# Block-sparse attention and FFN on one core: V's matmuls of DMA-turned visits moved to mid-step, queries on another queue

## The chip, the cores and the metric

The kernel runs on one core of one Trainium2 chip. The metric is the device time of one execution in microseconds, lower is better. PE, DVE, ACT and POOL are the compute engines (TensorE, VectorE, ScalarE, GpSimd); SP only issues DMAs here.

## The reference

For 4 batches, 8 heads, 768 positions and head size 64, attention is computed under a mask of 32 x 32 blocks: neighbours, the first and the last block row and column, and three sampled blocks per block row. The result, as 512 channels per position, goes through a layer norm, an FFN of 512 to 2048 to 512 with relu, and a residual.

```python
scores = np.where(mask, scale * q @ k.T, -1e9)
attn = np.exp(scores - scores.max(-1)); attn /= attn.sum(-1) + 1e-9
x = (attn @ v).transpose(0, 2, 1, 3).reshape(B, S, H * D)
xn = (x - mean) / np.sqrt(var + 1e-6) * g_ln
out = x + np.maximum(xn @ w_ch1, 0) @ w_ch2
```

## The kernel before

Each batch has six tiles of 128 queries, 24 tiles in all. A tile is worked through in visits: five tiles of a batch are one job "N" of two visits (four heads each, 256 gathered keys per block row); the tile with the edge blocks has a job "H" of one visit and a job "D" (dense rows) of four, where visits 0 and 1 are the two key halves of one set of heads, and 2 and 3 of the other. In order of work a batch is N, N, N, H, D, N, N: 15 visits, 60 in all, numbered through.

The main loop makes one step per visit (lines 564 to 620). In step s the scores of visit s run on PE (`scores`, L206) and their maximum on DVE (`biggest`, L242); then the V matmuls of the visit before, `pvi` (`attn_v`, L293), with their division on DVE (`evict`, L335 to L348); then the exponentials of visit s on ACT (`softmax`, L256). P has to be turned before V's matmuls. Either PE turns it within the step (`turn`: L283, copied out of PSUM by ACT, L284). Or, for visits marked `by_dma`, ACT and POOL split P in two f16 halves (L260, L261), SP issues two DMA transposes (`turn_begin`, L268), and in the next step DVE adds the turned halves (`turn_end`, L272). Marked are, from visit 9 on, the second half of the visits of N and D jobs.

FFN matmuls fill the rest of PE's time. A unit of two tiles (the first and the last unit have one) has 192 first-layer matmuls (L386; relu into f16 halves by ACT, L396, and DVE, L397) and 96 second-layer ones (L410), as f16 products in three terms, in three PSUM tiles. `run(amount)` emits matmuls up to a planned amount in ns (`yield c1`, 109 for two tiles, and `yield 215`). A unit may begin three steps after its last visit; `budget` spreads what is left over the steps until the next unit begins. The other work of a step is a list of tasks, and `run(budget / (len(tasks) + 1))` stands ahead of each: in the first visit of a job the next job's query load (`load_q`, L173, when it begins a tile), key steps (`keys`, on SP: one window load, then twelve gathers of 64 KB in four groups, L155) and V loads (`values`, L183 and L191 on ACT from job 7 on, else SP, and four gathers on POOL, L195); in the first steps the splitting of the weights (L441 to L452); then `turn`, and last `norms` (layer norm, and x turned by DMA transposes on SP, L367 xth and L368 xtl). Keys and V have two buffers each, so a load of V for the next job waits for the V matmuls of the job before this one.

Where `pvi` is a DMA visit, 2600 ns of FFN stand ahead of its V matmuls and beyond the budget:

```python
            if pvi.by_dma:
                turn_end(pvi)
                run(2600)
            attn_v(pvi)
```

Engines execute in the order in which the code emits to them, each queue for itself.

Of the kernel before, what the change touches and what calls it, by code (L numbers as in the profile page):

```python
# [25 lines left out]
def sparse_attention_moe(  # L26
# [13 lines left out]
    nc = tc.nc  # L40
# [7 lines left out]
    NX, LAG, FFN0 = 5, 1, 3  # L48
    LIFT = 2048.0
    BY_DMA = 9  # L50
# [8 lines left out]
    def ring(name, n, shape, dtype):  # L59
        return [const.tile(shape, dtype, name=f"{name}{i}") for i in range(n)]  # L60
# [10 lines left out]
    q_s = ring("q", 2, [P, 4, P], F32)  # L71
# [98 lines left out]
            nc.gpsimd.tensor_copy(kv[:, 0:n, s, :], src[:, m : m + 1, :].to_broadcast([P, n, P]))  # L170

    def load_q(n):
        nc.sync.dma_start(q_s[n % 2], qT[tiles[n].b, tiles[n].t])  # L173

    def values(job):
        src, vs = v[job.b], job.vs
# [76 lines left out]
    def softmax(vi):  # L253
        n, w = vi.shape
        for h in range(n):
            nc.scalar.activation(p_s[:, h * w : (h + 1) * w], seen(vi)[:, h, :], AF.Exp,  # L256
                                 bias=vi.st[:, 4 + h : 5 + h], scale=0.125)
            if vi.by_dma and (h + 1) % (n // 2) == 0:
                part = slice((h + 1 - n // 2) * w, (h + 1) * w)
                nc.scalar.copy(ph_s[:, part], p_s[:, part])  # L260
                nc.gpsimd.tensor_sub(pl_s[:, part], p_s[:, part], ph_s[:, part])  # L261
        if vi.kind == "D" and vi.r:
            nc.scalar.activation(vi.st[:, 12:16], vi.st[:, 8:12], AF.Exp)
# [6 lines left out]
    def turn_end(vi):  # L270
        c = vi.shape[0] * vi.shape[1] // P
        nc.vector.tensor_add(pt_s[vi.i % 2][:, 0:c, :], pth_s[:, 0:c, :], ptl_s[:, 0:c, :])  # L272
# [13 lines left out]
    def attn_v(vi):  # L286
        pt, vs = pt_s[vi.i % 2], vi.job.vs
        pv = vi.pv = ps_v.tile([P, 512], F32, tag="pv", name=f"pv{vi.i}")
        nch = 3 if vi.kind == "D" else 2
        begun = set()  # L290

        def mm(row, col, ch, vv, e, c):
            nc.tensor.matmul(pv[32 * row : 32 * row + 32, 65 * col : 65 * col + 65],  # L293
                             pt[:, ch, 32 * row : 32 * row + 32], vs[:, vv, 65 * e : 65 * e + 65],
                             start=row not in begun, stop=c == nch - 1, skip_group_check=True)
            begun.add(row)

        if vi.kind == "N":
            for h in vi.heads:
                for c in range(2):  # L300
                    for gg in range(4):
                        mm(gg, h % 4, (2 * (h % 2) + h % 4 // 2) * 2 + c, 2 * gg + c, h, c)
        elif vi.kind == "H":
            for pp in range(2):
                for j in range(2):
                    for c in range(2):
                        for rr in range(2):
                            h = 4 * pp + 2 * rr + j
                            for gg in range(2):
                                mm(2 * rr + gg, 2 * pp + j, (2 * j + pp) * 2 + c,  # L310
                                   2 * gg + c, h, c)
        else:
            for j in range(2):
                for c in range(3):
                    for rr in range(2):
                        for gg in range(2):
                            mm(2 * rr + gg, j, 3 * j + c, 3 * vi.r + c, 4 * vi.hf + 2 * rr + j, c)

    def evict(vi):
        n = 2 if vi.kind == "D" else 4  # L320
        u = vi.pv[:, 0 : n * 65].rearrange("p (h e) -> p h e", e=65)
        if vi.kind == "D":
            half = sm.tile([P, 2, 65], F32, tag="half", name=f"half{vi.i}")
            if not vi.r:
                nc.vector.tensor_copy(half, u)
                vi.half = half
                return
            wt = vi.st[:, 12:16].rearrange("p (r h) -> p r h", r=2).unsqueeze(3)
            nc.vector.tensor_mul(half, u, wt[:, 1].to_broadcast([P, 2, 65]))
            both = vi.mate.half  # L330
            nc.vector.tensor_mul(both, both, wt[:, 0].to_broadcast([P, 2, 65]))
            nc.vector.tensor_add(half, half, both)
            u = half
        rs = sm.tile([P, n, 1], F32, tag="rs", name=f"rs{vi.i}")
        nc.vector.tensor_scalar(out=rs, in0=u[:, :, D : D + 1], scalar1=1e-9 * LIFT,  # L335
                                scalar2=None, op0=ALU.add)
        nc.vector.reciprocal(rs, rs)
        x = vi.tile.x
        if vi.kind == "N":
            o = x[:, vi.hf * 256 : vi.hf * 256 + 256].rearrange("p (h d) -> p h d", d=D)  # L340
            nc.vector.tensor_mul(o, u[:, :, 0:D], rs.to_broadcast([P, 4, D]))
            return
        for rr in range(2):
            rows = slice(64 * rr, 64 * rr + 64)
            for pp in range(n // 2):
                h = 4 * (vi.hf if vi.kind == "D" else pp) + 2 * rr
                o = x[64:128, h * D : (h + 2) * D] if vi.kind == "D" else x[0:64, h * D : (h + 2) * D]
                nc.vector.tensor_mul(o.rearrange("p (j d) -> p j d", d=D),  # L348
                                     u[rows, 2 * pp : 2 * pp + 2, 0:D],
                                     rs[rows, 2 * pp : 2 * pp + 2, :].to_broadcast([64, 2, D]))  # L350
# [116 lines left out]
    tiles, units, visits = [], [], []  # L467
# [4 lines left out]
    n = 0  # L472
    while n < len(tiles):
        k = 1 if n == 0 or n == len(tiles) - 1 else 2
# [28 lines left out]
            for r in (1, 3):  # L503
                jobs[-1].visits[r].mate = jobs[-1].visits[r - 1]
    for vi in visits:
        vi.by_dma = vi.i >= BY_DMA and vi in vi.job.visits[len(vi.job.visits) // 2 :] and vi.kind != "H"
    NV = len(visits)
    NLAST = visits[-1].i

# [33 lines left out]
    def run(amount):  # L543
        while queue and (amount > 0 or queue[0].left <= 0):
            cost = next(queue[0].gen, None)
            if cost is None:
                queue.pop(0)
                continue
            if cost < 0:
                break  # L550
            queue[0].left -= cost
            amount -= cost

    def norms():
        for t in tiles:
# [3 lines left out]
            if t.normed is not None and t.spread is None:  # L559
                if t.u.i < 2 or units[t.u.i - 2].up_done:  # L560
                    norm_b(t)
                    t.spread = s

    while s < NV + LAG + 2 or queue or nextu < len(units):
        assert s < NV + 60
        vi = visits[s] if s < NV else None
        pvi = visits[s - LAG] if 0 <= s - LAG < NV else None
        if vi:
            scores(vi)
            biggest(vi)  # L570
        if pvi:
            t = pvi.tile
            if pvi is t.visits[0]:
                assert t.n < NX or tiles[t.n - NX].done
            if pvi.by_dma:
                turn_end(pvi)
                run(2600)
            attn_v(pvi)
            evict(pvi)
            if pvi is t.visits[-1]:  # L580
                t.ready = True
        if vi:
            softmax(vi)
            if vi.by_dma:
                turn_begin(vi)
        while nextu < len(units) and units[nextu].at <= s:
            u = units[nextu]
            if any(t.spread is None or t.spread >= s for t in u.tiles):
                break
            u.gen = ffn(u)  # L590
            u.left = 192 * (84, 109)[len(u.tiles) - 1] + 48 * 215 * len(u.tiles)
            queue.append(u)
            nextu += 1
        budget = 0
        if queue:
            left = sum(u.left for u in queue)
            budget = left / (max(1, units[nextu].at - s) if nextu < len(units) else 1)
        tasks = [(fn, args) for fn, args in todo.pop(s, [])]
        if vi:
            nxt = jobs[vi.job.i + 1] if vi is vi.job.visits[0] and vi.job.i + 1 < len(jobs) else None  # L600
            pre = []
            if nxt:
                gen = keys(nxt)
                pre = [(load_q, (nxt.visits[0].tile.n,))] if nxt.visits[0] is nxt.visits[0].tile.visits[0] else []
                pre += [(next, (gen, 0)), (values, (nxt,))] + [(next, (gen, 0))] * 6
            tasks = pre + tasks
            if queue:
                k = len(tasks) // 2
                tasks = tasks[:k] + [(turn, (vi,))] + tasks[k:]
            else:  # L610
                tasks = [(turn, (vi,))] + tasks
        tasks.append((norms, ()))
        for fn, args in tasks:
            run(budget / (len(tasks) + 1))
            fn(*args)
        if queue:
            want = sum(u.left for u in queue) - (left - budget)
            run(want)
        norms()
        s += 1  # L620
# [51 lines left out]
```

## Time and profile before

| | before |
|---|---|
| median of 3 runs | 835.66 us (835.5 to 836.88) |
| profiled execution | 833.35 us |
| its span, first to last instruction | 831.6 us |
| busy PE, DVE, ACT, POOL | 84%, 42%, 34%, 31% |
| TensorE clock granted, mean | 0.933 |

The profiled execution takes 1.75 us more than its span. In the profile's rows a line such as L293 is a line of the kernel; a row of the timeline has start, duration, engine, line, operation, output and input, and in brackets the idle time ahead of it and what ended it. Granted clock 1.00 is 2.4 GHz, 0.50 is 1.2 GHz.

### The profile page before, as it was taken

How to read it: one execution, taken by the hardware profiler on the slowest of the kernel's cores; microseconds unless marked ns; L12 is line 12 of the kernel's file. 1: busy time of each engine (PE TensorE's matmuls, PEld its weight loads, DVE VectorE, ACT ScalarE, POOL GpSimd, SP SyncE). 2: the span in 40 equal slices, each digit the busy share in tenths (PEclk: the TensorE clock that was granted, in tenths of full speed). 3: DMA queues.
4: the chain of work that ended last, by engine and by line, in shares of the span. 5: the costliest groups of instructions: out<-in, count | busy, mean ns of one | idle time of the engine just before them, and what ended most of it. 6: DMA issues, size and time to landing. Idle time of an engine off the chain costs nothing.

```text
span 831.6 us, 21737 instructions
## 1 busy us (share of the span) xinstructions
PE 702.6 (84%) x9160; PEld 461.9 (56%) x9160; DVE 351.7 (42%) x667; ACT 285.8 (34%) x577; POOL 261.4 (31%) x286
## 2 busy tenths in 40 slices
PE   0557374998599899997799999995998999996997
PEld 0225341764385675853674866742864857644764
DVE  2587876543233343443343333543324343542301
ACT  0456554432243242443242423433233423341200
POOL 5376447134323113234133203334233112321000
PEclk9956795999899999999799999998899999997999
DMA  8997768288967557399848357498776457663000
GB/s 332 269 327 225 246 243 242 48 200 220 214 135 194 141 145 209 102 225 238 228 124 201 88 179 231 122 216 207 192 179 166 87 184 202 160 114 52 13 26 13
DMA packets 158497, 144.22 MB, mean 173 GB/s; under 512 B 83264, under 2 KB 129600, under 8 KB 157376
## 3 DMA queue, kind: packets, MB, share of 16 engines
q1 hardware_dynamic: 134128, 73.62, 37.2%
q0 software_dynamic: 12416, 46.51, 17.3%
q10 hardware_dynamic: 11856, 22.71, 10.6%
q8 instruction: 72, 1.18, 0.6%
q14 instruction: 25, 0.20, 0.1%
HBM read 118.15 MB, written 6.29 MB: 150 GB/s over the span
## 4 chain that ended last, share of the span: by engine, by line
PE 59%; issue 13%; DMA 9%; DVE 7%; POOL 5%; SPq 3%; ACT 3%; POOLq 0%; ACTq 0%; DVEq 0%
PE pu L386 26%; PE pd L410 20%; PE pv L293 5%; PE ps L206 5%; DMA ks<-kT 4%; DMA stg<-stg 3%; PE pt L283 2%; DVE st L242 2%; DMA vs<-v 2%; POOL w2l L452 2%; DVE pt L272 1%; ACT p L256 1%; SPq L268 1%; ACT stg L260 1%; SPq L155 1%
## 5 line engine op out<-in xcount | busy, mean ns | idle before, releaser
L386 PEld LDWEIGHTS <-w1h 128*128 128x128 f16 x1664 | 154.7, 100 | 22.6 <-issue 3.4
L410 PE MATMUL pd<-w2l,hh 128*128 128x512 f16 x384 | 147.9, 385 | 6.3 <-POOL w2l L452 6.2
L410 PE MATMUL pd<-w2h,hh 128*128 128x512 f16 x384 | 147.6, 384 | 5.9 <-ACT w2h L451 5.9
L410 PE MATMUL pd<-w2h,hl 128*128 128x512 f16 x384 | 147.9, 385 | 0.0
L256 ACT ACTIVATE p<-ps,st 128x256 f32<-128x256 f32 (+1 forms) x208 | 88.3, 488 | 165.8 <-DVE st L244 127.2
L397 DVE SCALAR_TENSOR_TENSOR hl<-pu,hh 128x512 f16<-128x512 f32 x96 | 65.8, 690 | 170.5 <-ACT hh L396 170.5
L410 PEld LDWEIGHTS <-hh 128*128 128x128 f16 x768 | 75.6, 99 | 96.1 <-issue 14.5
L195 POOL DMA_INDIRECT vs<-v,rows x88 | 86.9, 988 | 124.5 <-PE pv L293 84.6
L386 PE MATMUL pu<-xth,w1h 128*128 128x256 f16 (+1 forms) x832 | 123.2, 270 | 0.0
L386 PE MATMUL pu<-xth,w1l 128*128 128x256 f16 (+1 forms) x832 | 122.4, 269 | 0.0
L386 PE MATMUL pu<-xtl,w1h 128*128 128x256 f16 (+1 forms) x832 | 120.5, 268 | 0.0
L396 ACT ACTIVATE hh<-pu 128x512 f16<-128x512 f32 x96 | 56.6, 595 | 172.4 <-PE pu L386 172.3
L206 PE MATMUL ps<-ks,q 64*32 64x256 f32 (+1 forms) x1664 | 80.9, 430 | 38.2 <-DMA ks<-kT 34.0
L293 PE MATMUL pv<-vs,pt 128*32 128x65 f32 x3584 | 70.0, 233 | 44.9 <-DVE pt L272 41.4
L242 DVE TENSOR_REDUCE st<-ps 128x4 f32<-128x1024 f32 (+1 forms) x60 | 69.0, 1151 | 89.7 <-PE ps L206 89.7
L293 PEld LDWEIGHTS pv<-vs,pt 128*32 128x32 f32 x3584 | 59.6, 117 | 75.4 <-issue 60.4
L261 POOL TENSOR_TENSOR stg<-p,stg 128x512 f16<-128x512 f32 (+1 forms) x50 | 53.9, 1078 | 112.7 <-issue 71.8
L386 PEld LDWEIGHTS <-w1l 128*128 128x128 f16 x832 | 78.6, 100 | 11.0 <-issue 1.6
L284 ACT COPY pt<-pt 128x512 f32<-128x512 f32 x70 | 36.3, 565 | 109.1 <-PE pt L283 86.0
L416 DVE SCALAR_TENSOR_TENSOR ot<-pd,x 128x512 f32<-128x512 f32 x24 | 16.6, 692 | 133.5 <-PE pd L410 131.3
L363 POOL TENSOR_TENSOR xl<-xn,xh 128x512 f16<-128x512 f32 x24 | 27.7, 1153 | 138.1 <-ACT xh L362 132.7
L206 PEld LDWEIGHTS ps<-ks,q 64*32 64x32 f32 x1664 | 29.2, 110 | 74.1 <-issue 57.1
(87 smaller groups left out, 531.9 us busy)
## 6 DMA issues: line engine op xcount, KB each, us to landing
ks<-kT SPq DMA_DIRECT2D x28, 768.0 KB
ks<-kT SPq DMA_DIRECT2D x264, 64.0 KB
vs<-v ACTq DMA_DIRECT2D x15, 780.0 KB
q<-qT SPq DMA_DIRECT2D x24, 256.0 KB
out<-ot POOLq DMA_DIRECT2D x24, 256.0 KB, 3.2
vs<-v ACTq DMA_DIRECT2D x3, 1560.0 KB
w2h<-w POOLq DMA_DIRECT2D x4, 1024.0 KB, 7.6
w2l<-w POOLq DMA_DIRECT2D x4, 1024.0 KB, 11.7
```

What stands on the lines that cost most here:

```text
L195: nc.gpsimd.indirect_dma_start(out=vs[:, 2 * gg, :], out_offset=None, in_=src, in_offset=bass.IndirectOffsetOnAxis(ap=rows[:, i : i + 1], ...
L206: nc.tensor.matmul(ps[32 * part : 32 * part + 32, col : col + n], lhs[64 * row : 64 * row + 64], rhs[64 * row : 64 * row + 64], start=True ...
L242: nc.vector.tensor_reduce(out=st[:, 0:n], in_=seen(vi), axis=AX.X, op=ALU.max, negate=True)
L256: nc.scalar.activation(p_s[:, h * w : (h + 1) * w], seen(vi)[:, h, :], AF.Exp, bias=vi.st[:, 4 + h : 5 + h], scale=0.125)
L261: nc.gpsimd.tensor_sub(pl_s[:, part], p_s[:, part], ph_s[:, part])
L284: nc.scalar.copy(dst[:, lo:hi, :], pt[:, 0 : hi - lo, :])
L293: nc.tensor.matmul(pv[32 * row : 32 * row + 32, 65 * col : 65 * col + 65], pt[:, ch, 32 * row : 32 * row + 32], vs[:, vv, 65 * e : 65 * e ...
L363: nc.gpsimd.tensor_sub(xl, xn, xh)
L386: nc.tensor.matmul(ph[:, j * n : (j + 1) * n], w[:, ct, fs], x[:, ct, 0:n], start=m == 0, stop=m == 3 * CT - 1, skip_group_check=True)
L396: nc.scalar.activation(dh, ph, AF.Relu)
L397: nc.vector.scalar_tensor_tensor(out=dl, in0=ph, scalar=0.0, in1=dh, op0=ALU.max, op1=ALU.subtract)
L410: nc.tensor.matmul(po, x[:, f, ts], w[:, f, :], start=m == 0, stop=m == 3 * FT - 1)
```

## The change

V's matmuls of a DMA visit are no longer emitted ahead of the step's exponentials but as one of the step's tasks (`values_in`): after the fourth key step in the first visit of a job, where the V loads of the next job then follow, and else after two empty tasks. The extra 2600 ns are gone. `turn` moves one place back, or behind `values_in`. Queries of tiles 5 and later are loaded on ACT's queue. Marked for DMA are, from visit 9 on, visits 1 of N jobs as before, and visits 1 and 3 of D jobs instead of 2 and 3.

```diff
     def load_q(n):
-        nc.sync.dma_start(q_s[n % 2], qT[tiles[n].b, tiles[n].t])
+        (nc.scalar if n > 4 else nc.sync).dma_start(q_s[n % 2], qT[tiles[n].b, tiles[n].t])
...
-        vi.by_dma = vi.i >= BY_DMA and vi in vi.job.visits[len(vi.job.visits) // 2 :] and vi.kind != "H"
+        vi.by_dma = vi.i >= BY_DMA and vi in vi.job.visits[1::2]
...
+    def values_in(vi):
+        t = vi.tile
+        if vi is t.visits[0]:
+            assert t.n < NX or tiles[t.n - NX].done
+        if vi.by_dma:
+            turn_end(vi)
+        attn_v(vi)
+        evict(vi)
+        if vi is t.visits[-1]:
+            t.ready = True
...
-        if pvi:
-            t = pvi.tile
-            if pvi is t.visits[0]:
-                assert t.n < NX or tiles[t.n - NX].done
-            if pvi.by_dma:
-                turn_end(pvi)
-                run(2600)
-            attn_v(pvi)
-            evict(pvi)
-            if pvi is t.visits[-1]:
-                t.ready = True
+        if pvi and not pvi.by_dma:
+            values_in(pvi)
...
+        mid = [(lambda: None, ())] * 2 + [(values_in, (pvi,))] if pvi and pvi.by_dma else []
...
-                pre += [(next, (gen, 0)), (values, (nxt,))] + [(next, (gen, 0))] * 6
-            tasks = pre + tasks
+                step = (next, (gen, 0))
+                if mid:
+                    pre += [step] * 4 + mid[2:] + [(values, (nxt,))] + [step] * 3
+                    mid = []
+                else:
+                    pre += [step, (values, (nxt,))] + [step] * 6
+            tasks = pre + mid + tasks
             if queue:
-                k = len(tasks) // 2
+                k = len(tasks) // 2 + (len(mid) or 1)
                 tasks = tasks[:k] + [(turn, (vi,))] + tasks[k:]
             else:
                 tasks = [(turn, (vi,))] + tasks
+        else:
+            tasks = mid + tasks
```

## Rows read from the trace of the kernel before

**Rows 1.** The page: busy time of engines, and the chain by engine.
```profile
PE 702.6 (84%) x9160; PEld 461.9 (56%) x9160; DVE 351.7 (42%) x667; ACT 285.8 (34%) x577; POOL 261.4 (31%) x286
...
PE 59%; issue 13%; DMA 9%; DVE 7%; POOL 5%; SPq 3%; ACT 3%; POOLq 0%; ACTq 0%; DVEq 0%
```

**Rows 2.** PE's waits from 145 us: us in total, times, longest us.
```profile
PE pv L293 <- DVE pt L272: 41.4, 11, 7.4
PE ps L206 <- DMA ks<-kT: 4.1, 4, 1.5
...
PE pv L293 <- ACT pt L284: 1.0, 1, 1.0
```

**Rows 3.** The timeline of PE: six rows with a wait ahead.
```profile
220.54 1.96 PE L293 MATMUL pv<-vs,pt 128*32 128x65 f32 x64 [6.50 <-DVE pt L272]
...
278.05 1.12 PE L293 MATMUL pv<-vs,pt 128*32 128x65 f32 x64 [2.82 <-DVE pt L272]
...
393.77 2.70 PE L206 MATMUL ps<-ks,q 64*32 64x256 f32 x24 [1.47 <-DMA ks<-kT]
400.81 1.96 PE L293 MATMUL pv<-vs,pt 128*32 128x65 f32 x64 [4.35 <-DVE pt L272]
...
741.58 1.12 PE L293 MATMUL pv<-vs,pt 128*32 128x65 f32 x64 [1.95 <-DVE pt L272]
...
759.77 1.96 PE L293 MATMUL pv<-vs,pt 128*32 128x65 f32 x64 [7.45 <-DVE pt L272]
```

**Rows 4.** Windows over the stretches: length, busy by engine, PEclk, DMA share, GB/s.
```profile
189.50:220.50 31.00, 18.93 (x275) 9.24 (x274) 10.39 (x18) 8.75 (x20) 10.88 (x14) 0.92 0.97 227
373.40:400.80 27.40, 17.97 (x275) 8.90 (x275) 10.38 (x18) 8.76 (x20) 10.84 (x14) 0.85 0.96 233
554.00:582.90 28.90, 17.49 (x275) 8.68 (x275) 10.49 (x18) 8.65 (x20) 10.78 (x14) 0.90 0.91 221
```

**Rows 5.** The timeline of SP's queue in steps 28 to 30.
```profile
375.00 1.45 SPq L173 DMA_DIRECT2D q<-qT  x1
...
379.68 6.66 SPq L155 DMA_DIRECT2D ks<-kT  x12
391.41 1.23 SPq L367 DMA_TRANSPOSE xth<-xh  x1
393.29 1.20 SPq L368 DMA_TRANSPOSE xtl<-xl  x1
394.60 2.88 SPq L268 DMA_TRANSPOSE stg<-stg  x2
```

**Rows 6.** The timeline of DVE: the add of visit 29's halves.
```profile
399.44 1.22 DVE L272 TENSOR_TENSOR pt<-stg 128x1024 f32<-128x1024 f16 x1 [1.51 <-DMA stg<-stg]
```

**Rows 7.** Windows at half clock, columns as in rows 4.
```profile
218.80:225.50 6.70, 4.96 (x79) 3.95 (x80) 1.99 (x4) 0.00 (x0) 2.38 (x3) 0.50 0.77 229
392.90:406.40 13.50, 8.29 (x106) 5.30 (x107) 3.38 (x6) 1.57 (x4) 5.09 (x7) 0.50 0.80 200
577.20:587.30 10.10, 5.04 (x80) 3.54 (x77) 3.38 (x6) 1.57 (x4) 1.95 (x2) 0.50 0.80 190
754.70:764.80 10.10, 5.03 (x79) 3.99 (x80) 1.99 (x4) 0.00 (x0) 0.00 (x0) 0.50 0.31 57
```

**Rows 8.** The timeline of PE: one D visit turned on PE.
```profile
149.57 0.82 PE L283 MATMUL pt<-id_sb,p 128*128 128x128 f32 x6
```

**Rows 9.** Timelines of PE and ACT around the end of step 5.
```profile
104.15 1.38 PE L293 MATMUL pv<-vs,pt 128*32 128x65 f32 x64 [2.37 <-ACT pt L284]
...
103.52 1.07 ACT L284 COPY pt<-pt 128x512 f32<-128x512 f32 x2
104.47 0.64 ACT L450 ACTIVATE ot<-ot 128x512 f32<-128x512 f32 x1
```

**Rows 10.** The timeline of ACT's queue in step 43: V's loads.
```profile
564.11 0.32 ACTq L183 DMA_DIRECT2D vs<-v  x1
567.72 0.32 ACTq L191 DMA_DIRECT2D vs<-v  x1
```

## The prediction

> **What bounds the kernel now.** I read the page first: PE is busy for 702.6 us and the chain that ended last is 59% PE, with 13% issue and 9% DMA behind it [rows 1]. So the time is PE's work plus what PE waits. The list of PE's waits from 145 us on, when the weights have been split, shows what these are: 41.4 us in 11 waits of V's matmuls (L293) for the add of the two turned halves of P (L272); keys come next with 4.1 us [rows 2]. The timeline of PE shows where they stand, and there are three kinds [rows 3]. In a short stretch before each new batch the V matmuls of steps 13 to 15, 28 to 30 and 43 to 45 wait; 220.54 (6.50 us) and 400.81 (4.35 us) are two of six, 23.5 us together (41.4 less the other five). At 278.05 a wait of 2.82 us stands where a unit has run out and the next isn't yet begun; there are three of this length, 8.5 us (steps 19, 34, 49). The last two, 1.95 and 7.45 us, stand in steps 58 and 60. Ahead of all these V matmuls PE has 2.6 us of FFN to run, or none.
>
> The windows over the three short stretches, from the start of step 13 (28, 43) to the V matmuls of visit 14 (29, 44), show PE busy 18.93 of 31.0, 17.97 of 27.4 and 17.49 of 28.9 us, and the DMA engines at 0.97, 0.96 and 0.91 [rows 4]. What ends such a stretch stands in SP's queue: it issues 12 key gathers, then issues nothing until 391.41, where it turns x (xth, xtl), and only then P's two halves at 394.60 [rows 5]; keys are still landing, scores wait for them until 393.77 [rows 3]; the add on DVE starts at 399.44, released by that DMA [rows 6]. So here P is late because SP stands behind keys that are under way; that it waits for them is my reading, no row here names it.
>
> **The change, step by step.** FFN matmuls carry planned costs of 109 and 215 ns, so a unit of two tiles is 192 x 109 + 96 x 215 = 41.6 us, spread over the steps until the next unit. Before, a step after a DMA visit spends 2.6 us of it ahead of V and beyond its budget; by the planner's sums steps 23 to 29 get 6.0, 6.0, 8.1, 7.5, 4.7, 7.5 and 1.7 us. After, nothing is taken ahead: 6.0, 6.0, 6.0, 7.3, 5.6, 5.4 and 5.4. V's matmuls then stand behind six of 13 slots where a new job's first visit has a new tile: 5.2 us of FFN in step 30 (budget 10.4), 2.6 in step 28.
>
> *Stretches before a batch.* Steps 28 and 29 carry 10.8 instead of 9.2 us, and 5.2 more stand ahead of V in step 30: 6.7 us more FFN before the same V matmuls. If SP's queue ends the stretch where it does now, this is work that PE does in time it idled, 6.7 us each; the idle time (31.0 - 18.93 and so on: 12.1, 9.4, 11.4 us, 32.9 together) has room. The FFN needs xtl of the newest tile: issued from 393.29 to 394.49 [rows 5], against scores that end at 396.47 [rows 3]; P needed 1.9 us from the end of its second issue (394.60 + 2.88 = 397.48) to 399.44, so by that xtl is in at about 396.4, just in time. Against it stands the clock: it was at 0.50 from 392.9 and from 577.2 on, before V's matmuls, and in the first stretch only from 218.8, inside the wait itself [rows 7]. FFN at half clock all through would take 10.4 us, a gain of 1.5; with all idle time gone it would be 11 on average. I take 6.7 for the first and 5 for the others, being nearer to the rows of SP: 16.7, between 4.5 and 32.9.
>
> *Half clock behind them.* At 0.50 PE was busy 4.96 us from 218.8, 5.6 from 400.8 (8.29 less 2.70 for scores) and 5.04 from 577.2 [rows 3, 7]; half of each is lost, 7.8 us. I take the first back, 2.5, as its wait goes; bounds 0 and 7.8. The Trainium skill (TensorE: Matmul & The Clock Gate, Part 1) says that throttled is the default state and activity lifts it. By that a PE kept at work would win all 7.8, and the sum would be 5.3 us better; the rows agree only that each of these stretches begins in or beside a wait.
>
> *Unit starts in steps 19, 34, 49.* The new unit's FFN (5.2 us) now stands ahead of the add, which needed 2.82 us: all goes, 8.5; I see no bound but 0 and 8.5, the low one if its x came late, and that was turned two steps earlier.
>
> *Steps 58 and 60.* Step 57 gets 0.9 us more and 0.4 more stand ahead of V in step 58: 1.95 falls by 1.3. In step 60, 12.7 us of the last pair's FFN stand ahead: 7.45 goes, and with it the half clock behind it, half of 5.03 us busy from 754.7 [rows 7]: 2.5. Together 11.3, between 7 and 12.
>
> *D visits.* Visits 1 and 3 instead of 2 and 3 go by DMA; the count per batch stays, except that visit 9 of the first batch is now turned on PE (visit 8 is too early): six transposes, 0.82 us [rows 8]. P of visit 23 has 6.0 us of step 23 and 3.3 of step 24 to arrive, where visit 24 had 6.0 and 2.6 before and no wait: nothing. Cost 0.8.
>
> *The turn on PE, one slot later.* Where a queue of FFN stands it moves by one task, mostly a key step. In step 5 that task is a weight split: pt's copies on ACT move behind the next L450, 0.64 us, the cast behind it and what these wait for, while V's matmuls at 104.15 had already waited 2.37 us for them [rows 9]. Bounds: 0 (DVE is later there) and 2.4; I take 0.5.
>
> *Queues.* Queries leave SP, where an issue held it up to 1.45 us [rows 5], and go to ACT behind the exponentials, 19 of them; 19 loads of V go from after the first to after the fourth key step, on ACT (one of them on SP), with POOL's four gathers behind them, waiting for V's matmuls as they do now. V is used two steps on, so a start later by half a step is covered by the whole step that follows, 5.4 us of FFN or more. On ACT, relu evictions and the norms' x are queued behind: the row shows L191 issuing at 567.72, 3.3 us after L183, held by a key DMA [rows 10]. PE has three PSUM tiles of 24 matmuls, 2.6 us each; two free ones cover a hold of 5.2 us. V's matmuls wait for ACT's copies 1.0 us now [rows 2], and these now stand ahead of the loads. Bounds: a gain of 1 and a loss of 10; I take a loss of 2. On DVE, relu's second half waits behind the add; the same two tiles cover it.
>
> Sum: 16.7 + 2.5 + 8.5 + 11.3 - 0.8 - 0.5 - 2 = 35.7. The profiled execution took 833.35, 1.75 more than its span and 2.31 under the median of 835.66. So 797.7 for its like, 800.0 for the median.
>
> **The rivals.** *DMA sets the stretches.* At 0.91 to 0.97 the engines have little room [rows 4]; shorter steps bring PE earlier to keys that come no earlier, and the wait moves from V to scores and x; then 16.7 and 2.5 fall away: 819. For it speaks that share; against it that SP was held, not the engines alone, and that the added FFN needs no DMA. The Trainium skill (DMA: Bandwidth & Descriptors, Issuing engines are not separate DMA queues) says that transfers from all issuing engines share the same 16 engines; by that, queries on ACT free SP's time and no bandwidth, and no row speaks against it.
>
> *All idle time goes.* SP, rid of queries, and V's loads, no longer waited for late, bring keys and P 3 us earlier; the stretches lose all 32.9 and the clock 7.8: 800 - 16.2 - 5.3 = 778.5. Against it: the DMA share again.
>
> *ACT becomes the bound.* Queries and V's loads each wait on ACT for the completion of key gathers issued just before; beyond 5.2 us PE runs out of PSUM tiles. The gain of 35.7 is gone at 35.7 / 19 = 1.9 us per job, a hold of 7.1 us, twice the 3.3 shown [rows 10]. At 8 us it is 19 x 2.8 = 53 us: 853. Against it: one wait of PE behind ACT in all of [rows 2].
>
> *Nothing changes.* Each wait is replaced by its like: 835.7.
>
> **The numbers.** The forecast has 0.62, DMA as the bound 0.18, all idle time 0.08, no change 0.04, ACT 0.08. Within the forecast a stretch term of 30 gives 787 and one of 4.5 gives 812; with the DMA case the range is 787 to 820, which leaves out 0.08 below and 0.12 above. Faster by over 0.2% (1.7 us, about what a measurement here can tell from no change): 0.88; within it 0.04; slower 0.08.
>
> **What would show it.** Right: waits on L272 fall from 41.4 to under 8 us, none of them at a unit start; at these, L386 runs ahead of L293; waits of scores for keys grow from 4.1 to some 10 us; the half clock at 218.8 and at 754.7 is gone. Wrong: V's matmuls still wait in steps 15, 30 and 45; the first FFN matmuls of a unit wait for xth or xtl; PE waits for L396 while ACT stands at L173, L183 or L191; or the stretches of [rows 4] grow.

## The result, and the profile after

The changed kernel takes 827.37 us (median of 4 runs, 826.09 to 830.32) against 836.27 us (835.5 to 837.92) for the kernel before on the same chip: a ratio of 0.9896, 95% interval 0.9861 to 0.993. It is faster, as forecast, but by 8.9 us where 35.7 were forecast, and outside the range of 787 to 820. The profiled executions took 828.61 and 833.35 us, their spans 826.9 and 831.6; the accounts below are in spans, 4.7 us apart.

On the page of the kernel after, PE is busy 705.8 us in 9166 matmuls, against 702.6 in 9160 before [rows 1]: the same work and six more transposes. Its waits from 145 us, answering to [rows 2]:

```profile
PE pv L293 <- DVE pt L272: 35.1, 14, 5.1
PE pu L386 <- DMA xth<-xh: 6.7, 3, 3.0
PE ps L206 <- DMA ks<-kT: 2.1, 1, 2.1
```

V's matmuls still wait 35.1 us for the add, where under 8 were forecast. But these are other waits than before. The timeline of PE after shows the kinds:

```profile
280.77 1.11 PE L293 MATMUL pv<-vs,pt 128*32 128x65 f32 x64 [2.64 <-DVE pt L272]
...
342.02 0.89 PE L293 MATMUL pv<-vs,pt 128*32 128x65 f32 x48 [1.18 <-DVE pt L272]
...
361.27 1.53 PE L293 MATMUL pv<-vs,pt 128*32 128x65 f32 x48 [3.38 <-DVE pt L272]
...
404.32 0.60 PE L386 MATMUL pu<-xtl,w1h 128*128 128x256 f16 x4
407.55 1.45 PE L293 MATMUL pv<-vs,pt 128*32 128x65 f32 x64 [2.63 <-DVE pt L272]
...
770.25 1.11 PE L293 MATMUL pv<-vs,pt 128*32 128x65 f32 x64 [0.25 <-DVE pt L272]
```

At all six unit starts that have V of a DMA visit (steps 15, 19, 30, 34, 45, 49; 280.77 and 407.55 are two) the wait is 2.63 or 2.64 us, 15.8 together. Steps 24, 39 and 54 wait 1.18 to 1.19 (342.02), and steps 11, 26, 41 and 56, the last dense visit's V, 3.38 to 5.09 (361.27), 15.4 together; before, none of these seven steps had a wait. The 7.45 us in step 60 have become 0.25 (770.25), and the waits of steps 13, 28, 43 and 58 are gone. A wait so equal in six places with different traffic isn't a transfer's. The view of line L272 says so: what its engine sat idle for ahead of the add, first before, then after:

```profile
  DMA stg<-stg: 22.5, 8
```

```profile
its engine sat idle before it (us, times) until:
who waited for it (us, times):
```

Before, DVE stood idle eight times, 22.5 us, until P's transpose landed; after, never: no row stands under that heading. Something on DVE's own queue stands ahead of the add. ACT, then DVE, in the timeline of step 30, just ahead of the V matmuls at 407.55:

```profile
404.95 0.60 ACT L396 ACTIVATE hh<-pu 128x512 f16<-128x512 f32 x1 [2.02 <-PE pu L386]
```

```profile
405.58 0.69 DVE L397 SCALAR_TENSOR_TENSOR hl<-pu,hh 128x512 f16<-128x512 f32 x1 [1.93 <-ACT hh L396]
406.19 1.22 DVE L272 TENSOR_TENSOR pt<-stg 128x1024 f32<-128x1024 f16 x1
```

`values_in` emits the add directly ahead of V's matmuls, so behind the FFN of that step. The last FFN matmul ends at 404.92; ACT's half of relu takes 0.60, DVE's half 0.69, and the add 1.22, with small gaps 2.63 us, in which no matmul runs on PE. At these unit starts the FFN ahead of V is 48 matmuls (in step 30 from 399.35 on), exactly two PSUM tiles, and so the last tile ends right ahead of V. I call this theory A: the add waits behind the eviction of the FFN that was to hide it (the copying of its PSUM tile through relu). Theory B, its rival, is that P's turned halves come late from DMA.

In steps 11, 26, 41 and 56 the relu ahead of the add is itself late. In step 26 its tile had ended at 355.59, but ACT's half started only at 359.01, behind exponentials that ran from 357.57. In step 56 two tiles are late in this way, and ahead of the second one's half ACT stood idle 1.84 us, with a query load in between. So by these rows a part of this wait, at 5.09 us the longest, comes from the queries that the change put on ACT:

```profile
723.42 0.35 ACTq L173 DMA_DIRECT2D q<-qT  x1
723.82 0.60 ACT L396 ACTIVATE hh<-pu 128x512 f16<-128x512 f32 x1 [1.84 <-DMA ks<-kT]
```

Where the time went shows in windows by groups of steps, up to step 13, then by turns steps 13 to 15, 16 to 27 and so on, and from step 58. Columns: window, length, busy us and number of second-layer matmuls (L410) on PE and of their weight loads, clock, DMA share and GB/s. Before, after, and experiment e1 below:

```profile
0.00:189.50 189.50, 28.34 (x102) 10.47 (x102) 0.83 0.79 235
189.50:235.40 45.90, 11.50 (x43) 4.27 (x42) 0.89 0.93 222
235.40:373.40 138.00, 55.24 (x246) 23.43 (x246) 1.00 0.64 161
373.40:416.00 42.60, 9.81 (x43) 3.87 (x42) 0.84 0.91 231
416.00:554.00 138.00, 55.27 (x246) 23.42 (x246) 1.00 0.63 161
554.00:597.50 43.50, 9.78 (x43) 3.86 (x42) 0.88 0.89 228
597.50:735.30 137.80, 55.04 (x245) 23.31 (x245) 1.00 0.64 162
735.30:831.60 96.30, 41.41 (x188) 18.04 (x187) 0.94 0.15 31
```

```profile
0.00:194.20 194.20, 26.02 (x90) 9.28 (x90) 0.82 0.79 231
194.20:233.00 38.80, 12.39 (x55) 5.04 (x54) 0.96 0.91 220
233.00:377.50 144.50, 53.62 (x234) 22.65 (x234) 0.96 0.69 163
377.50:416.40 38.90, 12.36 (x55) 5.04 (x54) 0.96 0.99 221
416.40:556.40 140.00, 52.45 (x234) 22.32 (x234) 1.00 0.70 168
556.40:596.90 40.50, 12.43 (x55) 5.04 (x54) 0.92 0.87 216
596.90:740.90 144.00, 54.15 (x238) 22.68 (x238) 0.99 0.66 160
740.90:826.90 86.00, 42.95 (x195) 18.71 (x194) 0.99 0.15 35
```

```profile
0.00:188.80 188.80, 24.80 (x90) 9.03 (x90) 0.83 0.80 235
188.80:229.20 40.40, 12.37 (x55) 5.03 (x54) 0.92 0.89 216
229.20:362.30 133.10, 52.48 (x234) 22.28 (x234) 1.00 0.74 176
362.30:401.60 39.30, 12.40 (x55) 5.03 (x54) 0.96 1.02 222
401.60:534.80 133.20, 52.54 (x234) 22.30 (x234) 1.00 0.70 176
534.80:571.90 37.10, 12.34 (x54) 5.04 (x54) 1.00 0.91 231
571.90:705.50 133.60, 53.52 (x238) 22.64 (x238) 1.00 0.70 176
705.50:792.40 86.90, 42.93 (x195) 18.72 (x194) 0.98 0.16 36
```

From before to after: the start +4.7; the three groups ahead of and around a new batch -7.1, -3.7 and -3.0, although each holds 12 L410 (2.6 us) more; the three groups between +6.5, +2.0 and +6.2, although they hold 12, 12 and 7 fewer; the end -10.3. Sum -4.7. The first-layer matmuls (L386) are the same in number in each group. So two forecast gains came in, and the middle of each batch gave most of them back. In the first of these middles the kernel after has two windows at half clock (columns as in [rows 4]):

```profile
281.80:285.20 3.40, 3.40 (x24) 2.89 (x18) 0.77 (x3) 0.59 (x1) 2.00 (x2) 0.51 0.32 88
360.30:367.20 6.90, 5.93 (x65) 4.21 (x66) 4.88 (x13) 1.81 (x4) 1.89 (x2) 0.51 0.70 199
```

They stand just behind the wait that ends at 280.77 and across the end of the one at 361.27. With them the terms close: 4.4 us more of waits (7.2 against 2.8), half of 3.40 + 5.93 for the clock, 4.7, less 2.6 of FFN: 6.5, as measured. The second middle group, whose clock stayed at 1.00, has 4.4 less 2.6: 1.8, measured 2.0.

### The profile page after: what moved, and what is told of

Its sections match the earlier page's. It is cut to its first block, busy times and chain, and to the rows that moved or that the text cites. A ratio compares the mean times of both kernels' runs of the same rounds, so it can differ in the third digit from the quotient of the medians.

```text
span 826.9 us, 21725 instructions
## 1 busy us (share of the span) xinstructions
PE 705.8 (85%) x9166; PEld 465.7 (56%) x9166; DVE 346.4 (42%) x666; ACT 287.7 (35%) x577; POOL 260.3 (31%) x284
## 3 DMA queue, kind: packets, MB, share of 16 engines
q8 instruction: 72, 1.18, 0.6%
## 4 chain that ended last, share of the span: by engine, by line
PE 59%; issue 13%; DMA 9%; DVE 7%; POOL 4%; ACT 4%; SPq 2%; ACTq 0%; POOLq 0%; another core or an unknown queue 0%
PE pu L386 24%; PE pd L410 21%; PE pv L293 6%; PE ps L206 5%; DMA ks<-kT 4%; PE pt L283 3%; DMA xth<-xh 3%; DMA vs<-v 2%; DVE pt L272 2%; DVE st L242 2%; POOL w2l L452 2%; ACT p L256 1%; ACT hh L396 1%; SPq L155 1%; POOL vs L195 1%
## 5 line engine op out<-in xcount | busy, mean ns | idle before, releaser
L386 PEld LDWEIGHTS <-w1h 128*128 128x128 f16 x1664 | 153.8, 100 | 32.0 <-issue 13.1
L410 PE MATMUL pd<-w2h,hh 128*128 128x512 f16 x384 | 148.2, 386 | 7.6 <-ACT w2h L451 7.6
L410 PE MATMUL pd<-w2l,hh 128*128 128x512 f16 x384 | 147.4, 384 | 5.4 <-POOL w2l L452 5.2
L410 PE MATMUL pd<-w2h,hl 128*128 128x512 f16 x384 | 147.8, 385 | 0.0
L410 PEld LDWEIGHTS <-hh 128*128 128x128 f16 x768 | 75.1, 99 | 96.3 <-issue 13.4
L386 PE MATMUL pu<-xth,w1h 128*128 128x256 f16 (+1 forms) x832 | 122.8, 270 | 6.7 <-DMA xth<-xh 6.7
L386 PE MATMUL pu<-xtl,w1h 128*128 128x256 f16 (+1 forms) x832 | 122.3, 268 | 1.2 <-DMA xtl<-xl 1.2
L386 PE MATMUL pu<-xth,w1l 128*128 128x256 f16 (+1 forms) x832 | 122.5, 270 | 0.0
L293 PE MATMUL pv<-vs,pt 128*32 128x65 f32 x3584 | 71.6, 233 | 41.5 <-DVE pt L272 35.1
L206 PE MATMUL ps<-ks,q 64*32 64x256 f32 (+1 forms) x1664 | 77.0, 422 | 32.0 <-DMA ks<-kT 31.8
L386 PEld LDWEIGHTS <-w1l 128*128 128x128 f16 x832 | 79.4, 100 | 11.0 <-issue 1.9
L261 POOL TENSOR_TENSOR stg<-p,stg 128x512 f16<-128x512 f32 (+1 forms) x48 | 52.2, 1087 | 96.1 <-ACT stg L260 70.2
L284 ACT COPY pt<-pt 128x512 f32<-128x512 f32 x72 | 38.5, 562 | 122.5 <-PE pt L283 92.5
L416 DVE SCALAR_TENSOR_TENSOR ot<-pd,x 128x512 f32<-128x512 f32 x24 | 16.6, 692 | 124.8 <-PE pd L410 124.8
L410 PEld LDWEIGHTS <-hl 128*128 128x128 f16 x384 | 37.9, 99 | 49.2 <-issue 7.1
```

Of the source, the lines that this page charges most:

```text
L206: nc.tensor.matmul(ps[32 * part : 32 * part + 32, col : col + n], lhs[64 * row : 64 * row + 64], rhs[64 * row : 64 * row + 64], start=True ...
L284: nc.scalar.copy(dst[:, lo:hi, :], pt[:, 0 : hi - lo, :])
L386: nc.tensor.matmul(ph[:, j * n : (j + 1) * n], w[:, ct, fs], x[:, ct, 0:n], start=m == 0, stop=m == 3 * CT - 1, skip_group_check=True)
L410: nc.tensor.matmul(po, x[:, f, ts], w[:, f, :], start=m == 0, stop=m == 3 * FT - 1)
```

## The experiments

Edits are against the kernel after, where not said otherwise; ratios are to the kernel before, with 95% intervals.

**The add at the head of the step (e1)**, where it stood before; only V's matmuls stay mid-step.

```diff
-        if vi.by_dma:
-            turn_end(vi)
         attn_v(vi)
...
-        if pvi and not pvi.by_dma:
+        if pvi and pvi.by_dma:
+            turn_end(pvi)
+        elif pvi:
             values_in(pvi)
```

> The changed kernel, but the add of P's halves (L272) is emitted at the head of the step, right behind the maximum, ahead of all FFN; V's matmuls stay mid-step. Theory A (the add stood on DVE behind the relu half of the FFN tile just ended, so V's matmuls wait for PE's last FFN matmul, ACT, DVE and the add in a row, 2.6 us each time): the 14 waits of V's matmuls, 35.1 us, fall below 10 us, and the time to 800 to 812 us. Theory B (P's halves themselves come late from DMA): the add waits on DVE instead, the relu halves queue behind it and PE waits for PSUM tiles; the time stays at 823 to 832 us.

Measured: 795.73 us, 0.9516 (0.9463 to 0.9568). The waits of PE from 145 us:

```profile
PE pu L386 <- DMA xth<-xh: 6.1, 2, 3.4
PE pv L293 <- DVE pt L272: 4.7, 6, 1.7
PE ps L206 <- DMA ks<-kT: 3.3, 2, 3.0
```

The order of one add is worth some 32 us against the kernel after, 4 us more than the best that I expected: theory A holds. Theory B is right in that P does come late, but not in what this costs. DVE stands idle for it again, nearly as long as in the kernel before, but PE has FFN to run meanwhile; the view of L272, with the time that DVE sat idle ahead of it:

```profile
  DMA stg<-stg: 21.5, 10
```

In the windows of e1 above, against those after, the middle groups are 28.6 us shorter, the start 5.4, the groups around a batch only 1.4 (116.8 against 118.2), and the end is 0.9 longer. In step 30 the add and V's matmuls now stand so:

```profile
392.41 1.23 DVE L272 TENSOR_TENSOR pt<-stg 128x1024 f32<-128x1024 f16 x1 [3.08 <-DMA stg<-stg]
```

```profile
386.26 1.61 PE L206 MATMUL ps<-ks,q 64*32 64x256 f32 x20 [3.04 <-DMA ks<-kT]
...
394.22 1.11 PE L293 MATMUL pv<-vs,pt 128*32 128x65 f32 x64
```

The add is released by the transfer and done at 393.64, under FFN, 0.6 us ahead of V. But the scores of the same step wait 3.04 us for keys: here, taking V's wait away only uncovers the DMA's.

**The add two or three tasks ahead of V (e2)**, so behind some of the FFN; it leaves `values_in` as in e1.

```diff
-        mid = [(lambda: None, ())] * 2 + [(values_in, (pvi,))] if pvi and pvi.by_dma else []
+        mid = [(turn_end, (pvi,)), (lambda: None, ()), (values_in, (pvi,))] if pvi and pvi.by_dma else []
...
+                    both = (lambda: (next(gen, 0), turn_end(pvi)), ())
+                    pre += [step, both, step, step] + mid[2:] + [(values, (nxt,))] + [step] * 3
```

> The changed kernel, but the add is emitted two or three FFN slots ahead of V's matmuls instead of directly ahead. Theory A: the waits of 2.6 us vanish wherever the FFN between lasts 2 us or more (unit starts, steps 15 to 22 and their like), those of 1.2 us in D steps too; 35.1 us falls below 12 us, time 803 to 814 us, and where P is late this is better than the add at the head of the step, since DVE isn't held as long. Theory B: no more than 5 us of the waits go, 822 to 830 us.

Measured: 805.43 us, 0.9624 (0.9573 to 0.9675), V's waits 16.6 us in 8. The time is as expected, the waits are not: below 12 us were. Those at the unit starts of steps 19, 34 and 49 fell to 0.36 us, those of steps 30 and 45 are gone, those of steps 11, 26, 41 and 56 stayed at 2.64 to 3.39. In step 26 the rows still show relu's half on DVE directly ahead of the add, and so the wait stays. Step 15 has one of 2.81 us of the other kind: there DVE stood idle for 2.70 us until P landed. The head of the step is the better place.

**1300 ns of FFN between the add and V (e12)**: if the wait is a chain of 2.63 us, half its length of other work must leave half of it.

```diff
             turn_end(vi)
+            run(1300)
```

> The changed kernel with 1300 ns of FFN (12 first-layer matmuls) between the add and V's matmuls, the add staying behind the FFN as in the change. Theory A, refined (the wait is 2.6 us from the end of the last FFN tile to the end of the add, less the FFN that stands in between): each of the 14 waits falls by up to 1.3 us: six of 2.63 to 1.3, three of 1.2 to none, the four of 3.4 to 5.1 to about 2.1 to 3.8; 35.1 us becomes 17 to 21 us and the time 808 to 815. Theory B (P late): no change, 823 to 830.

Measured: 829.63 us, 0.9919 (0.9886 to 0.9953). All six waits at unit starts are now 1.32 or 1.33 us; the one of step 19:

```profile
279.07 1.11 PE L293 MATMUL pv<-vs,pt 128*32 128x65 f32 x64 [1.33 <-DVE pt L272]
```

So the length of the wait is settled. The time missed its forecast, because other waits grew (30.4 us in 15 waits altogether, against 35.1 in 14). In steps 24, 39 and 54 V waits 1.70 to 3.70 us, and now for P itself; DVE in step 24:

```profile
340.15 0.96 DVE L272 TENSOR_TENSOR pt<-stg 128x768 f32<-128x768 f16 x1 [3.73 <-DMA stg<-stg]
```

In steps 26 and 41 it waits 4.68 and 4.74 us; there ACT stood idle 3.46 and 3.52 us ahead of its half of relu, with a query load in between, as in step 56 above. The 1300 ns are spent beyond the budget and so are lacking in later steps; that this is what brought both about fits, but isn't shown.

**The kernel before with the add behind its 2600 ns (e10)**: does the order alone make the wait there too?

```diff
             if pvi.by_dma:
-                turn_end(pvi)
                 run(2600)
+                turn_end(pvi)
             attn_v(pvi)
```

> The kernel before with two lines swapped: the add is emitted behind the 2600 ns of FFN that stand ahead of V's matmuls, not ahead of them. Nothing else. Theory A: 18 of 25 DMA visits have that FFN; in each V's matmuls now wait for the add, 1.2 us, and where a first-layer PSUM tile has just ended also for ACT's and DVE's relu, 2.6 us; less what the short steps wait already, 15 to 40 us slower: 851 to 876. Theory B (only P's arrival counts): 834 to 840.

Measured: 841.38 us, 1.0057 (1.0032 to 1.0083): slower, but far less than I expected. Eight new waits of 0.33 to 0.80 us, 4.4 together, stand in the dense jobs' steps and are nearly the loss of 4.8 (841.38 against 836.63 for the kernel before, run beside it); the N jobs' steps have none. So the order alone doesn't make a wait of 2.63 us everywhere. The trace of the run shows what else it takes. In step 25 a first-layer tile ends at 350.75, relu's half stands on DVE directly ahead of the add, and 14 more first-layer matmuls cover all but 0.75 us of the chain. In step 17, of an N job, the FFN ahead of V is of the second layer (L410), behind which no relu comes, and V doesn't wait. So it takes a first-layer tile that ends right ahead of V for the whole chain to become a wait.

**Only the last V moved (e11)**: the kernel before, with V of visit 59 in step 60 behind two empty tasks, everything else as before.

```diff
+        if pvi and not vi:
+            tasks = [(lambda: None, ())] * 2 + [(last_in, (pvi,))] + tasks
```

> The kernel before, with only the very last V matmuls (visit 59, in step 60) put behind two empty tasks, so that the last pair's FFN stands ahead of them. The prediction's term for it: a wait of 7.45 us and 2.5 us of half clock go, 825 to 829 against 836. If this term is most of what the whole change won (about 9 us), the rest of the change is worth nothing by itself. If the wait comes back elsewhere: 833 to 837.

Measured: 827.58 us, 0.9886 (0.9836 to 0.9936), the wait in step 60 is 0.25 us. One move in one step gives what the whole change gives (0.9896): the rest of the change nets nothing, gains around each batch against losses in its middle.

**The dense visits alone (e4)**, visits 1 and 3 marked in the kernel before.

> The kernel before, with one part of the change alone: visits 1 and 3 of D jobs are turned by DMA instead of 2 and 3. I hold it for nearly nothing: 1 us slower for visit 9's transposes on PE, 835 to 838 us against 836. A rival: DMA visits that no longer follow each other free the single buffer of P's halves earlier, and 2600 ns ahead of V's matmuls move to other steps; then 3 to 6 us either way.

Measured: 846.95 us, 1.0128 (1.0084 to 1.0172), some 10 us slower; both expectations missed. V's waits are 48.6 us in 18. SP's queue and then DVE around step 24:

```profile
327.60 10.91 SPq L155 DMA_DIRECT2D ks<-kT  x12
338.62 3.46 SPq L268 DMA_TRANSPOSE stg<-stg  x2
```

```profile
343.65 0.96 DVE L272 TENSOR_TENSOR pt<-stg 128x768 f32<-128x768 f16 x1 [3.99 <-DMA stg<-stg]
```

The V matmuls behind this add waited 3.55 us. P of visit 23 stands on SP behind the twelve key gathers of the next job: POOL had finished its halves at 335.25, and SP was at the gathers until 338.51. P of visit 24, a step later, met none in the kernel before. 2.6 us of FFN don't cover such a hold.

**The queries alone (e5)**, in the kernel before.

> The kernel before, with queries of tiles 5 and later on ACT's queue alone. If SP's time is what holds P in the short stretches, keys, x and P come about 1 us earlier in each: waits for the add fall from 41.4 to some 36 us, 829 to 833 us. If completion of the transfers holds them, the time stays within 2 us of 836. If ACT is held by the issue, 838 or more.

Measured: 839.29 us, 1.0026 (0.9991 to 1.0061): no difference that can be told.

**e1 without the other two parts**: with dense visits 2 and 3 as before (e6), with queries on SP (e7), and with both (e13).

> The changed kernel with the add at the head of the step, but D visits 2 and 3 turned by DMA as before, not 1 and 3. D visits 1 and 3 alone had cost 1.3%, with three added waits of 1.3 to 3.6 us per kernel half a step after the exponentials. If that cost is one of V's matmuls standing too early, it is gone with V at mid-step and this is within 3 us of 796. If the marks themselves cost (the split and turning collide with other work), it gives 5 us or more back: under 791.

> The changed kernel with the add at the head of the step, but all queries on SP as before. Queries on ACT alone moved nothing (ratio 1.0026, interval across 1). Expected the same here: within 3 us of 796. A rival: with the waits for P gone, SP's queue decides the keys and x of the short stretches, and queries on SP cost 1 us in each, 799 to 802.

> V's matmuls at mid-step with the add at the head of the step, and nothing else of the change (D visits 2 and 3, queries on SP). If the other two parts add nothing, 792 to 797, as the three kernels that have the add at the head and one or both of them. If queries on SP and D visits 2 and 3 together cost, 798 or more.

Measured: 794.19 us, 0.9489 (0.9463 to 0.9515); 795.89 us, 0.9513 (0.9484 to 0.9542); 794.55 us, 0.9513 (0.9463 to 0.9562). With e1's, the four can't be told apart: V's matmuls mid-step with the add at the head is all that wins, some 41 us, and neither the queries nor the choice of dense visits adds anything that can be told. All four beat both kernels. In e13 V's waits are 6.4 us and the scores' waits for keys 10.6.

**V mid-step without the other two parts (e8)**, the add directly ahead of V. In this kernel the turn of a dense job's visit 3 is issued into the buffer of visit 2's turned P before the add of visit 2 reads it, so V of visit 2 is multiplied by P of visit 3.

> The change's main part alone: V's matmuls of DMA visits at mid-step, the add directly ahead of them, with D visits 2 and 3 and all queries on SP as before. Theory A: its waits are those of the whole change, 824 to 830, since the other two parts are worth nothing once V stands at mid-step. A rival: D visits 1 and 3, 1.3% slower by themselves, cost here too, and it is 816 to 822.

Measured: 847.05 us, 1.0129 (1.0077 to 1.018). The add of visit 2 waits for visit 3's turn, and V's matmuls with it, 5.3 to 5.6 us in the dense steps, so the time says nothing of the placement alone. But the six unit starts, which have no dense visit's V, wait 2.63 or 2.64 us here too. And the run shows why visits 1 and 3 belong to a late add: no two visits in a row then share the buffer.

**The norms earlier (e9)**: e1, with x turned after the fifth key step of a job's first visit.

```diff
-                    pre += [step] * 4 + mid[2:] + [(values, (nxt,))] + [step] * 3
+                    pre += [step] * 4 + mid[2:] + [(values, (nxt,)), (lambda: (next(gen, 0), norms()), ())] + [step] * 2
```

> The changed kernel with the add at the head of the step, and the layer norm of a tile that became ready emitted two tasks earlier in a job's first visit, one key step after V's matmuls. What is left there is 6 us in which the first FFN matmuls of a unit wait for turned x. If its norm is what is late, 2 to 4 us of these go: 791 to 795. If SP's queue is full with keys until then, nothing: 795 to 798.

Measured: 800.13 us, 0.9558 (0.9537 to 0.958), no better than e1. FFN's waits for x fell from 6.1 to 4.0 us, the scores' for keys rose from 3.3 to 6.6. The wait changed its place and not its size. Together the two come to 9.4 us in e1, 8.1 in e6, 8.9 in e7, 11.3 in e13 and 10.6 here; that suggests that around a batch the transfers set the end now.

## Why the prediction was wrong, point by point

*The step that failed* is the one on unit starts, "The new unit's FFN (5.2 us) now stands ahead of the add, which needed 2.82 us: all goes, 8.5", with its like on the queues, "On DVE, relu's second half waits behind the add". Both see FFN ahead of the add as cover. But FFN ahead of the add on PE puts FFN's relu ahead of it on DVE: the add waits behind relu, not relu behind the add. The waits of steps 19, 34 and 49 went from 2.82 to 2.63 us, 0.6 in place of 8.5, and steps 15, 30 and 45 wait the same 2.63. Of the 35.1 us that V's matmuls wait, all but some 0.3 are this and its like in the dense steps below. The forecast costed the order of one queue, PE's, for a move that changed the order of two.

*Dense visits*, forecast as nothing: 3.6 us of new waits in steps 24, 39 and 54 and 15.4 in steps 11, 26, 41 and 56, from the same order, made longer in the last four by what stood ahead of relu on ACT. That P had time to arrive was true in the changed kernel, where the add never made DVE wait for it; by itself, in e4, it was not, since the text counted the steps and not SP's queue.

*Stretches before a batch and the clock behind them*, forecast 16.7 + 2.5 = 19.2. The three groups are 13.8 us shorter with 36 more L410, 7.7 us at the planned 215 ns: 21.5 in all. The term was right, and its reason half so. V's wait there did not go, it is 2.63 us in each; and with it gone in e1 the groups gain only 1.4 us more, since PE's idle time in them stays, 16.5 us against 16.9. In e1 PE waits 9.4 us there for xth and keys (8.8 after), V's matmuls wait 3.3 for adds in steps 13, 28 and 43, and for another 3.8, mostly ahead of V's matmuls too, the profile names no releaser. The windows after that answer to [rows 4]:

```profile
194.20:224.40 30.20, 24.77 (x335) 14.37 (x334) 12.60 (x21) 10.16 (x22) 10.93 (x13) 0.99 0.98 232
377.50:407.50 30.00, 24.40 (x335) 14.34 (x334) 12.40 (x21) 10.16 (x22) 10.97 (x13) 1.00 1.06 229
556.40:587.90 31.50, 25.83 (x335) 15.01 (x334) 12.17 (x21) 10.06 (x22) 10.90 (x13) 0.95 0.92 227
```

PE is busy 25.0 us on average in place of 18.1, so 6.9 more, near the 6.7 us of FFN of the forecast, and the windows are 30.6 us long in place of 29.1. The rival that DMA sets the stretches had the next bound right (6.7 us of waits for xth, 2.1 for keys), and the loss of 19.2 us that it drew from it wrong.

*Half clock* at the end is gone as forecast, 0.94 to 0.99 in the last window, and less in the groups around a batch (0.89, 0.84 and 0.88 before, 0.96, 0.96 and 0.92 after; what that gave is within the 21.5). But the first middle group, at 1.00 before, is at 0.96. In e1, without these waits, it is 1.00 again. So a wait put where there was none can cost the clock too: here it did, while waits of the same length left the second middle group at 1.00.

*Steps 58 and 60*, forecast 11.3: the end is 10.3 us shorter with 7 more L410, 1.5 us: 11.8. Right, and e11 shows the part of step 60 alone.

*Visit 9 and the turn a slot later*, forecast 1.3 of cost: in e1 the start is 0.7 us shorter with 12 fewer L410, 2.6: a cost of 1.9. Near as a sum, but the term of the turn, 0.5, was too small: in step 5 V's matmuls waited 4.47 us for ACT's copies after and 4.83 in e1, against 2.37 before, so 2.1 and 2.5 more, near the upper bound of 2.4. What made up for it wasn't looked into. The 4.7 us after have the wait of step 11 (3.57) on top, and behind it a granted clock of 0.76 from 179 to 186 us.

*Queues*, forecast 2 of loss: e5 and e7 show nothing that can be told. The list of PE's waits names ACT nowhere from 145 us on, and the rival of ACT as the bound, a price of 53 us, fell. But a trace of its mechanism is there: ACT's half of relu held at a query load, in step 56 (1.84 us) and in e12, reached PE through the add.

*The sum without the step that failed.* With the add at the head, V's matmuls wait only 4.7 us for it (the forecast had under 8), and the kernel takes 795.73 us where 800.0 was forecast. The windows let the terms be compared, e1 against before, with L410 at 215 ns: around a batch 22.7 us gained (forecast 19.2), in the middles 7.2 (8.5), at the end 10.9 (11.3), at the start 1.9 lost (1.3), for the queues nothing (2 lost). So the closeness is not mere luck, though the first term was right for only half of its reason. The sum fits a kernel with the add ahead of the FFN; the change put the add behind it.

## What to carry to other kernels

Moving an instruction's place on one engine moves what it depends on among other engines' queues: list, for each engine, what will stand ahead of it there, and what that in turn waits for. Here filler work hid a short operation where that stood ahead of the filler's own evictions (e1); directly behind them it hid nothing of it. So emit the add at the head and its consumer mid-step. And read a wait's length: here the same 2.63 us in six places was a chain of instructions, not a transfer, and what the add's own engine idled for told which.

## What was not expected of the hardware

A turn of x took far longer to land than the 1.9 us by which the forecast had placed it (an estimate from P's turn). SP's queue, and PE, after:

```profile
390.20 1.77 SPq L367 DMA_TRANSPOSE xth<-xh  x1
```

```profile
399.35 0.60 PE L386 MATMUL pu<-xth,w1h 128*128 128x256 f16 x4 [2.95 <-DMA xth<-xh]
```

From the issue's end at 391.97 to the start of the matmul that by the profile waited for it are 7.4 us, in a window whose DMA share was 1.06. Why this one is slower than P's wasn't tried.
